# An S5 state-space layer beside a SwiGLU feed-forward layer: the last chunk's state output by seven block products, and the program's end in another order

## The chip, the core and the metric

The kernel runs on one core of a Trainium2 chip. The metric is device time in microseconds (us), lower is better. The engines are TensorE (PE in the profile, its weight loads PEld), VectorE (DVE), ScalarE (ACT), GpSimd (POOL) and SyncE (SP, which here only starts DMAs). Each engine runs its own instructions in order; what it needs from another engine it waits for.

## The reference

For 2048 rows `x` of 512 values, in bfloat16:

```python
xn = layernorm(x)
Lam_bar = exp(dt * Lam)                                  # Lam, B, C are complex, 512 states
h[t] = Lam_bar * h[t-1] + B_bar @ xn[t]                  # a recurrence over the 2048 rows
state = 2 * real(h @ C.T) + xn * Dskip
ffn = (silu(xn @ w_gate) * (xn @ w_up)) @ w_down         # 1376 features
out = x + state + ffn
```

## The kernel before

**Chunks and tiles.** The rows are worked in four chunks of 512 (`c` = 0 to 3), each of four tiles of 128 rows (`n` = 0 to 15). For a chunk the kernel projects to the states (`bproj_tile`), turns by the phase so that the recurrence becomes real (`rotation`, `rotation_dma`), scans along the rows on DVE (line 473, `g`), turns back into `wt` (real and imaginary part as two planes), and multiplies `wt` by `CF`, which holds the output matrix. `rotation_dma` does a part of the turning by DMAs that add into SBUF (line 438: `u<-pm`, `wt<-pm`). Beside this run the gate and up projections (line 508) into `gu_tiles[c]`, called `guT` in the profile, and their product on DVE (line 523).

**The output of a tile** is collected in one bank of PSUM, of which there are eight (`bank()`, tile name `ps`): ten matmuls of the feed-forward layer over 1280 features (`wd_sb`), three more over 32 rows of the array for the last 96 features (`out_rows`, with `gu_rows`), and the state output. `o_tiles[n]` is the list of the banks of tile `n`; `out_blocks` cuts one tile into column blocks of 256, 128 and 128, so that its stores can start one after the other.

**Seven products.** The state output of a chunk is a product of a 512 by 1024 matrix (`wt`, blocks `a11` to `a22`: time halves by planes) with a 1024 by 512 matrix (blocks `b11` to `b22`). For chunks 0, 1 and 2 `out_ssm_seven` makes it from seven block products instead of eight, with sums of blocks beforehand (`s1` to `s4` of `wt`, `t1` to `t4` of `CF`) and sums of products behind:

| name in the text | product | goes to |
|---|---|---|
| one | a11 b11 | own bank, copied to SBUF by ACT (line 731) |
| six | s2 t2 | own bank; six + one = u2 |
| five (`x`) | s1 t1 | own bank, copied to SBUF by ACT (line 734); five + u2 = low half, right |
| seven | s3 t3 | own bank; seven + u2 = high half, left; that + five = high half, right |
| low-left, high-left, low-right | a12 b21, a22 t4, s4 b22 | straight into the banks of the tiles |

Each product is eight matmuls 128x256. "Low" are a chunk's first two tiles, "high" the other two. The sums of products are DVE additions of 128x2x256 float32 (line 710). At the end DVE adds a tile's bank and the matching sum into `res`, which is stored. `skipped` adds `xn*Dskip + x`, kept in `xall`, to the sums of chunk 2 on POOL (line 717). Chunk 3 has no block sums: `out_ssm` multiplies the whole `wt` by `CF`, eight matmuls 128x512 a tile (line 815).

**The end of the program** is `out_pair(2)`, written out by hand: the feed-forward matmuls of all eight tiles of chunks 2 and 3 (line 779), their `out_rows`, the seven products of chunk 2, and then the plain state output of chunk 3, whose last tile (15) is cut in blocks. To free two banks before that, DVE first adds the banks of tiles 14 and 15 to `xn_end` and keeps them in `ends` (line 787). The block sums of chunk 2 (`state_sums(2)`: two copies on the ACT queue, four negations on ACT, four adding DMAs on the POOL queue) are started behind the first of the eight tiles.

**Order elsewhere.** Most of DVE's work for the recurrence waits in a list, `backlog`; `step()` issues its next item, `pump(us)` issues items as PE work of that length is recorded, `need(tag)` issues all up to a tag. `sums` is a second list, of which `spend(n)` issues up to cost `n` behind each gate and up tile.

Of the kernel before, what the change touches and what calls it, by code (L numbers as in the profile page):

```python
# [10 lines left out]
F32 = mybir.dt.float32  # L11
# [12 lines left out]
def kernel(  # L24
# [144 lines left out]
    part_end, jidx = ends[:, 0, :], ends[:, 1, :]  # L169
# [427 lines left out]

    def out_blocks(n):

        return ((0, D // 2), (D // 2, D - 128), (D - 128, D)) if n == NT - 1 else ((0, D),)  # L600

    def out_rows(c, step):

        for i in range(TPC):
            n, rows = c * TPC + i, slice(i * RT, (i + 1) * RT)
            nc.tensor.matmul(o_tiles[n][0][:], lhsT=gu_rows[c][rows, step, :], rhs=wd_rows[rows, step, :],  # L606
                             start=False, stop=(step == 2 and (c == 0 or n in parts)))
# [3 lines left out]
    parts = {NT - 1: part_end, NT - 2: jidx}  # L611
# [38 lines left out]
    def state_places(c):  # L650
        if c == 0:
            return halves(xnT, 0) + halves(xnT, 1)
        if c == 1:
            return [ssm.tile([128, NQ, HW], BF16, name="cm", bufs=3) for _ in range(2)] + halves(xnT, 2)
        return halves(wg_g[2], 0) + halves(wu_g[2], 0)

    def state_sums(c):

        (a11, a12), (a21, a22) = state_quarters(c)
        s1, s2, s3, s4 = s_tiles[c] = [t[:] for t in state_places(c)]  # L660
        q = nc.scalar if c == 2 else nc.sync
        if c == 0:
            yield from negated(s2, a22)
        yield from copied(s4, a12, q)
        yield from copied(s1, a21, q)
        yield from negated(s3, a21)
        yield from added(s3, a11)
        if c == 1:
            yield None
        if c:  # L670
            yield from negated(s2, a22)
        yield from added(s1, a22)
        if c == 0:
            yield None
        yield from added(s2, s3)
        yield from added(s4, s2)

    def out_ssm_seven(c, meanwhile=()):

        (a11, a12), (a21, a22) = state_quarters(c)  # L680
        (b11, b12), (b21, b22) = BQ
        (s1, s2, s3, s4), (t1, t2, t3, t4) = s_tiles[c], TQ
        first = c * TPC
        if c == 0:
            space = u_all[:].rearrange("p a b j -> p (a b j)").bitcast(F32).rearrange("p (s j) -> p s j", j=HD)
            spots = (0, 4)
            five = ssm.tile([128, D], F32, name="cm", bufs=3)[:].rearrange("p (i j) -> p i j", i=2)
        else:
            space = flat(gu_tiles[c][:]).bitcast(F32).rearrange("p (s j) -> p s j", j=HD)
            spots = (2, 6)  # L690
            five = space[:, 0:2]
        high, low = (space[:, a:a + 4].rearrange("p (i h) j -> p i h j", h=2) for a in spots)
        u2 = high[:, :, 1]

        def product(a, b, place, start, stop):
            for i in range(2):
                for q in range(NQ):
                    nc.tensor.matmul(place(i), lhsT=a[:, q, i * 128:(i + 1) * 128], rhs=b[:, q, :],  # L698
                                     start=(start and q == 0), stop=(stop and q == NQ - 1))

        def at(half, h):
            return lambda i: o_tiles[first + 2 * half + i][0][:, h * HD:(h + 1) * HD]

        def taken(a, b):
            x = bank((128, 2, HD))
            product(a, b, lambda i: x[:, i, :], True, True)
            return x

        def add(out, in0, in1):
            V.tensor_tensor(out=out, in0=in0, in1=in1, op=ALU.add)  # L710
            owed[0] -= 0.69

        def skipped(half, extra):
            if c == NCH - 2:
                lo = first + 2 * half
                sums = extra.rearrange("p i h j -> p i (h j)")
                nc.gpsimd.tensor_tensor(out=sums, in0=sums, in1=xall[:, lo:lo + 2, :], op=ALU.add)

        def finish(half, extra):
            for i in range(2):  # L720
                n = first + 2 * half + i
                res = opool.tile([128, D], BF16, name="res")
                add(res[:], o_tiles[n][0][:], extra[:, i].rearrange("p h j -> p (h j)"))
                if c == NCH - 2:
                    nc.sync.dma_start(out=out_v[:, n, :], in_=res[:])
                else:
                    nc.gpsimd.dma_start(out=out_v[:, n, :], in_=res[:], accum_op=ALU.add)  # L727

        product(a12, b21, at(0, 0), False, False)
        one = taken(a11, b11)  # L730
        nc.scalar.copy(out=low[:, :, 0], in_=one[:])  # L731
        six = taken(s2, t2)
        x = taken(s1, t1)
        nc.scalar.copy(out=five, in_=x[:])
        for _, op in meanwhile:
            op()

        def between():
            if c < NCH - 2:
                step()  # L740

        between()
        add(u2, six[:], low[:, :, 0])
        seven = taken(s3, t3)
        add(low[:, :, 1], u2, five)
        skipped(0, low)
        product(a22, t4, at(1, 0), False, c > 0)
        between()
        add(high[:, :, 0], seven[:], u2)
        add(high[:, :, 1], high[:, :, 0], five)  # L750
        skipped(1, high)
        product(s4, b22, at(0, 1), False, c > 0)
        if c == 0:
            for k in range(3):
                out_rows(c, k)
        between()
        if c == NCH - 2:
            finish(0, low)
            return lambda: finish(1, high)
        finish(1, high)  # L760
        finish(0, low)
        pump(4 * 2 * NQ * 0.2163)

    def out_pair(c):

        multiply(0)
        for n in [*parts, *range(c * TPC, NT - len(parts))]:
            o_tiles[n] = [bank()]
        for n in range(c * TPC, (c + 2) * TPC):
            if n == c * TPC + 1:  # L770
                need("skip")
                for _, op in filter(None, state_sums(c)):
                    op()
                skip_store(0)
                skip_store(1)
            o = o_tiles[n][0]
            k, i = divmod(n, TPC)
            for fi in range(FT - 1):
                nc.tensor.matmul(o[:], lhsT=gu_tiles[k][:, fi, i * 128:(i + 1) * 128], rhs=wd_sb[:, fi, :],  # L779
                                 start=(fi == 0), stop=False)  # L780
            pump(FT * 0.2163)
        for step in range(3):
            for k in (c, c + 1):
                out_rows(k, step)
        need(f"ssm{c + 1}")
        for n, part in parts.items():
            V.tensor_tensor(out=part, in0=o_tiles[n][0][:], in1=xn_end[:, n - NT + TPC, :], op=ALU.add)
        rest = out_ssm_seven(c)
        for n in range((c + 1) * TPC, (c + 2) * TPC):
            if n in parts:  # L790
                o_tiles[n] = [bank((128, hi - lo)) for lo, hi in out_blocks(n)]
            out_ssm(n)
            if n == NT - TPC:
                rest()

    def out_ffn(n):
        c, i = divmod(n, TPC)
        o_tiles[n] = []
        for lo, hi in out_blocks(n):
            o = bank((128, hi - lo))  # L800
            o_tiles[n].append(o)
            for fi in range(FT - 1):
                nc.tensor.matmul(o[:], lhsT=gu_tiles[c][:, fi, i * 128:(i + 1) * 128], rhs=wd_sb[:, fi, lo:hi],  # L803
                                 start=(fi == 0), stop=False)

    def out_ssm(n):
        c, i = divmod(n, TPC)
        if c > 0:
            res = opool.tile([128, D], BF16, name="res")
        for o, (lo, hi) in zip(o_tiles[n], out_blocks(n)):  # L810
            fresh = n in parts
            o = o[:, 0:hi - lo]
            for part in range(2):
                for q in range(NQ):
                    nc.tensor.matmul(o, lhsT=w_tiles[c][:, part, q, i * 128:(i + 1) * 128],  # L815
                                     rhs=CF[:, part, q, lo:hi], start=(fresh and part == 0 and q == 0),
                                     stop=(c > 0 and part == 1 and q == NQ - 1))
            if c == NCH - 1:
                rest = parts[n][:, lo:hi] if fresh else xn_end[:, i, lo:hi]
                V.tensor_tensor(out=res[:, lo:hi], in0=o, in1=rest, op=ALU.add)  # L820
# [367 lines left out]
```

## Time and profile before

| | |
|---|---|
| median of three runs | 176.35 us (176.21 to 176.76) |
| the profiled execution's own time | 176.91 us, of which the profile's span is 175.1 us |
| PE busy | 171.7 us, 98% of the span, granted clock 1.00 |
| DVE busy | 154.9 us, 88% |
| ACT busy | 100.3 us, 57% |
| POOL busy | 68.8 us, 39% |
| start of the feed-forward output matmuls of chunk 2 (line 779) | 140.44 us |
| last matmul's part of the chain ends | 172.44 us |

The profile is of one execution; it took 1.81 us more than its span, and lies 0.56 us above the median of the three runs. A row of the timeline gives the start, the length, the engine, the line and the operation with its tiles and shapes; in brackets stands how long the engine had been idle and what ended that. Matmuls overlap in the profile: one of 128x512 is shown with 379 ns, though the next starts 216 ns later. So a start is the better measure on PE, and a short wait doesn't show as idle time.

### The profile page before, as it was taken

To read this page: it belongs to the slowest core of one execution; us is meant where nothing else is said; L and a number is where in the kernel's file an instruction comes from. 1 tells how busy PE (TensorE), PEld (TensorE's weight loads), DVE (VectorE), ACT (ScalarE), POOL (GpSimd) and SP (SyncE) were. 2 spreads that over 40 slices of the span, in tenths; PEclk is the share of its full clock that TensorE was granted. 3 is DMA by queue.
4 is the path that set the end of the run, shared out by engine and by line. 5 is a ranking of instruction groups with operands and counts; after the bars stand their busy time and mean duration, and the time that the engine had idled before them with its cause. 6 is when DMAs were issued, how large, how long until landed. Compare 5 with 4: busy or idle time off the path is not lost.

```text
span 175.1 us, 2875 instructions
## 1 busy us (share of the span) xinstructions
PE 171.7 (98%) x1026; PEld 90.6 (52%) x1026; DVE 154.9 (88%) x223; ACT 100.3 (57%) x190; POOL 68.8 (39%) x87
## 2 busy tenths in 40 slices
PE   8999999999999999999999999999999999999993
PEld 3977644444444444444444584468444444447743
DVE  3778999999999998999999959997999999943884
ACT  5487899869997899199767760002297614001100
POOL 7050499312043314344520052595475003544440
DMA  5998498997574999999990669596999995949934
GB/s 170 300 164 210 95 260 118 340 198 150 106 212 144 172 168 247 190 140 124 115 117 7 181 88 105 64 140 112 170 135 197 159 146 132 105 53 131 173 99 140
DMA packets 45758, 26.61 MB, mean 152 GB/s; under 512 B 22272, under 2 KB 44544, under 8 KB 45728
## 3 DMA queue, kind: packets, MB, share of 16 engines
q0 software_dynamic: 12624, 11.67, 48.7%
q1 hardware_dynamic: 30672, 13.61, 34.6%
q10 hardware_dynamic: 2448, 1.15, 2.8%
q8 instruction: 8, 0.13, 0.3%
q14 instruction: 6, 0.05, 0.1%
HBM read 8.33 MB, written 4.19 MB: 71 GB/s over the span
## 4 chain that ended last, share of the span: by engine, by line
PE 98%; DVE 0%; issue 0%
PE ps L508 36%; PE ps L393 16%; PE ps L698 11%; PE ps L803 10%; PE ps L779 10%; PE ps L815 4%; PE ps L909 3%; PE ps L886 2%; PE ps L561 2%; PE ps L990 2%; PE ps L606 2%; PE ps L553 1%; PE ps L245 1%; DVE res L820 0%; PE ps L275 0%
## 5 line engine op out<-in xcount | busy, mean ns | idle before, releaser
L508 PE MATMUL ps<-xnT,wg 128*128 128x512 bf16 (+1 forms) x148 | 36.6, 373 | 0.0
L508 PE MATMUL ps<-xnT,wu 128*128 128x512 bf16 (+1 forms) x148 | 36.6, 373 | 0.0
L473 DVE TENSOR_TENSOR_SCAN g<-r_t,car,u 128x512 bf16<-128x512 f32 x24 | 29.1, 1266 | 0.0
L393 PE MATMUL ps<-xnT,BT 128*128 128x512 bf16 x128 | 28.3, 379 | 0.0
L527 ACT ACTIVATE guT<-ps 128x512 bf16<-128x512 f32 (+1 forms) x40 | 24.0, 601 | 6.4 <-PE ps L508 3.2
L528 ACT CAST u_all<-ps 128x512 bf16<-128x512 f32 (+1 forms) x40 | 23.3, 584 | 5.1 <-PE ps L508 4.8
L508 PEld LDWEIGHTS <-wu 128*128 128x128 bf16 x148 | 14.5, 98 | 16.6
L508 PEld LDWEIGHTS <-wg 128*128 128x128 bf16 x148 | 14.5, 98 | 16.5
L395 ACT CAST u<-ps 128x512 bf16<-128x512 f32 x32 | 18.3, 587 | 3.9 <-PE ps L393 3.7
L393 PEld LDWEIGHTS <-BT 128*128 128x128 bf16 x128 | 12.3, 98 | 15.2 <-issue 0.8
L803 PE MATMUL ps<-wd_sb,guT 128*128 128x512 bf16 x80 | 17.6, 379 | 0.0
L779 PE MATMUL ps<-wd_sb,guT 128*128 128x512 bf16 x80 | 17.4, 379 | 0.0
L731 ACT COPY guT<-ps 128x512 f32<-128x512 f32 x2 | 1.2, 585 | 27.0 <-PE ps L698 27.0
L523 DVE TENSOR_TENSOR guT<-guT,u_all 128x1024 bf16<-128x1024 bf16 x20 | 13.3, 677 | 0.0
L803 PEld LDWEIGHTS <-guT 128*128 128x128 bf16 x80 | 7.8, 98 | 9.6 <-issue 0.4
L779 PEld LDWEIGHTS <-guT 128*128 128x128 bf16 x80 | 7.8, 98 | 9.5
L205 DVE BATCH_NORM_STATS2 stats<-xall 128x6 f32<-128x512 bf16 x14 | 9.4, 674 | 2.7 <-DMA xall<-in_A_x_dram 2.7
L214 POOL TENSOR_TENSOR rstd<-ve,neg_half 128x2 f32<-128x2 f32 (+1 forms) x4 | 5.1, 1287 | 15.5 <-DVE ve L213 15.5
L625 POOL DMA_DIRECT2D xnT<-wt x3 | 3.9, 1287 | 15.2 <-DMA cm<-wt 12.0
L473 DVE TENSOR_TENSOR_SCAN g<-r_t,u 128x512 bf16<-128x512 f32 x8 | 9.3, 1204 | 0.0
L727 POOL DMA_DIRECT2D out_dram<-res x8 | 7.7, 1590 | 2.2 <-DVE res L710 2.2
L698 PEld LDWEIGHTS <-wt 128*128 128x128 bf16 x72 | 6.9, 98 | 1.8 <-issue 0.8
(180 smaller groups left out, 291.0 us busy)
## 6 DMA issues: line engine op xcount, KB each, us to landing
wt<-pm POOLq DMA_DIRECT2D x4, 512.0 KB, 5.7
u<-pm POOLq DMA_DIRECT2D x4, 512.0 KB, 6.3
wd_sb<-in_B_w_down_dram SPq DMA_DIRECT2D x2, 640.0 KB, 9.9
xall<-in_A_x_dram SPq DMA_DIRECT2D x1, 1024.0 KB, 6.7
out_dram<-res POOLq DMA_DIRECT2D x8, 128.0 KB, 4.9
out_dram<-xall POOLq DMA_DIRECT2D x2, 512.0 KB, 8.4
xnT<-wt SPq DMA_DIRECT2D x3, 256.0 KB, 3.7
xnT<-wt POOLq DMA_DIRECT2D x3, 256.0 KB, 7.0
```

What stands on the lines that cost most here:

```text
L205: nc.vector.bn_stats(out=stats[:, n, :], in_=xall[:, n, :])
L393: nc.tensor.matmul(ps[:], lhsT=BT[:, part, k, q * 128:(q + 1) * 128], rhs=xnT[:, k, c * CW:(c + 1) * CW], start=(k == 0), stop=(k == KD - 1))
L395: nc.scalar.copy(out=u_tiles[c][:, part, q, :], in_=ps[:])
L473: V.tensor_tensor_scan(out=g()[:, part, q, :], data0=r_t[:, q:q + 1].to_broadcast([128, CW]), data1=u_tiles[c][:, part, q, :], initial=ini ...
L508: nc.tensor.matmul(ps[:fs, lo:hi], lhsT=wslice(groups, fi, k), rhs=xnT[:, k, c * CW + lo:c * CW + hi], start=(k == 0), stop=(k == KD - 1))
L523: products.append(lambda: V.tensor_tensor(out=g, in0=g, in1=u, op=ALU.mult))
L527: nc.scalar.activation(out=gu_tile(c)[:, fi, 0:hi], in_=psg[:, 0:hi], func=ACT.Silu)
L528: nc.scalar.copy(out=u_tile(c, fi)[:, fi % 2, 0:hi], in_=psu[:, 0:hi])
L698: nc.tensor.matmul(place(i), lhsT=a[:, q, i * 128:(i + 1) * 128], rhs=b[:, q, :], start=(start and q == 0), stop=(stop and q == NQ - 1))
L727: nc.gpsimd.dma_start(out=out_v[:, n, :], in_=res[:], accum_op=ALU.add)
L779: nc.tensor.matmul(o[:], lhsT=gu_tiles[k][:, fi, i * 128:(i + 1) * 128], rhs=wd_sb[:, fi, :], start=(fi == 0), stop=False)
L803: nc.tensor.matmul(o[:], lhsT=gu_tiles[c][:, fi, i * 128:(i + 1) * 128], rhs=wd_sb[:, fi, lo:hi], start=(fi == 0), stop=False)
```

## The change

The state output of chunk 3 is made by seven block products like the other three chunks, and `out_pair` is replaced by `out_last`. In the new order PE does the feed-forward output of six tiles (the four of chunk 2, then 14 and 15 of chunk 3), then the products of chunk 2 and of chunk 3, the `out_rows` of both chunks, and last the feed-forward output of tiles 12 and 13. The tile cut in blocks is 13 (`LAST`) instead of 15.

The block sums of chunk 3 are four DVE additions (`state_sums_dve`), placed between DVE's sums of products. Those of chunk 2 are started earlier, during the gate and up projections of chunk 3: their two copies go to SP's queue, ahead of the twelve small DMAs that bring `gu_rows` of chunk 3, and their negations go between ACT's work for the gate and up tiles; they lie in `xnT` instead of `wg`/`wu`. `skip_add` and `skip_store` go behind some of them on POOL's queue. In all four chunks five stays in its bank and DVE reads it from there; ACT's copy of it is gone. In `out_ssm_seven(0)` one more `step()` is issued ahead of the first sum. The keeping of tiles 14 and 15 in `ends` is gone; tiles 14 and 15 keep their banks, and `skipped` is done for chunk 3 too.

```diff
     def state_sums(c):
...
+        if c == 2:
+            yield 1, lambda: None
+            yield from negated(s2, a22)
...
+    def state_sums_dve(c):
+        (a11, a12), (a21, a22) = state_quarters(c)
+        s1, s2, s3, s4 = s_tiles[c] = state_places(c)
+        for out, in0, in1, op in ((s3, a11, a21, ALU.subtract), (s1, a21, a22, ALU.add), (s2, s3, a22, ALU.subtract),
+                                  (s4, a12, s2, ALU.add)):
+            yield lambda out=out, in0=in0, in1=in1, op=op: V.tensor_tensor(out=out, in0=in0, in1=in1, op=op)
...
-        nc.scalar.copy(out=five, in_=x[:])
...
+        def add_low(self):
+            self.add(self.low[:, :, 1], self.p5[:], self.u2)
...
     def out_ssm_seven(c, meanwhile=()):
...
+        for _ in range(2 - c):
+            step()
+        p.add_six()
...
-    def out_pair(c):
+    def out_last(c):
         multiply(0)
+        need("skip")
+        late = [op for op in leftover if op]
+        for _, op in late[:1]:
+            op()
+        skip_store(2)
+        for _, op in late[1:]:
+            op()
+        skip_add()
+        skip_store(0)
+        skip_store(1)
+        lo, hi = c * TPC, (c + 1) * TPC
+        for n in (*range(lo, hi), hi + 2, hi + 3):
+            out_ffn(n)
             pump(FT * 0.2163)
+        need(f"ssm{c + 1}")
+        sums = state_sums_dve(c + 1)
+        p = Seven(c)
+        p.one()
+        p.six()
+        p.x()
+        next(sums)()
+        next(sums)()
+        p.add_six()
+        next(sums)()
+        p.seven()
+        p.add_seven()
+        p.add_low()
+        p.skipped(0)
+        p.add_high()
+        p.skipped(1)
+        p.low_left()
+        r = Seven(c + 1)
+        r.one()
+        r.six()
+        r.x()
+        next(sums)()
+        r.add_six()
+        r.seven()
+        r.add_seven()
+        r.add_low()
+        r.add_high()
+        r.skipped(1)
+        r.skipped(0)
+        p.high_left()
+        p.low_right()
         for step in range(3):
+            out_rows(c, step, closes=range(lo, hi))
+        for i in range(TPC):
+            p.finish(i)
+        open_tile(hi)
+        open_tile(LAST)
+        for step in range(3):
+            out_rows(c + 1, step, opens=(hi, LAST))
+        r.high_left(closes=True)
+        r.finish(2, (nc.scalar,), 2)
+        r.finish(3)
+        for i in range(2):
+            r.low_left(only=(i,))
+            r.low_right(only=(i,))
+        out_ffn(hi)
+        r.finish(0, (nc.scalar,))
+        out_ffn(LAST)
+        r.finish(1, (nc.scalar, nc.scalar, nc.sync))
...
     out_chunk(1)
+    need("ssm2")
+    third = state_sums(2)
+    sums += iter(lambda: next(third), None)
+    leftover[:] = third
     gateup_chunk(3)
-    out_pair(2)
+    spend(99)
+    out_last(2)
```

`p` is the product object of chunk 2 and `r` that of chunk 3; `finish(i)` is the last addition of the chunk's tile `i` and its store.

**DVE, its end, before.** From the last scans of chunk 3 (`g`) over the turning back into `wt` to the sums of products of chunk 2 (`guT`) and the last additions:

```order
L413 TENSOR_TENSOR wt<-pm 128x2048
L403 TENSOR_TENSOR pm<-g,c_91 128x2048
L417 TENSOR_TENSOR wt<-pm 128x2048
L787 TENSOR_TENSOR ends<-ps,xn_end 128x512 x2
L710 TENSOR_TENSOR guT<-ps,guT 128x2x256
L710 TENSOR_TENSOR guT<-guT 128x2x256
L710 TENSOR_TENSOR guT<-ps,guT 128x2x256
L710 TENSOR_TENSOR guT<-guT 128x2x256
L710 TENSOR_TENSOR res<-ps,guT 128x512 x2
```

**DVE, its end, now.** `wu` and `wg` are the block sums of chunk 3 in the order s3, s1, s2, s4; `guT` are sums of products of chunk 2 and `u` those of chunk 3:

```order
L417 TENSOR_TENSOR wt<-pm 128x2048
L699 TENSOR_TENSOR wu_82<-wt 128x4x256
L699 TENSOR_TENSOR wg_81<-wt 128x4x256
L743 TENSOR_TENSOR guT<-ps,guT 128x2x256
L699 TENSOR_TENSOR wg_81<-wu_82,wt 128x4x256
L743 TENSOR_TENSOR guT<-ps,guT 128x2x256 x3
L699 TENSOR_TENSOR wu_82<-wt,wg_81 128x4x256
L743 TENSOR_TENSOR u_1874<-ps,u_1874 128x2x256 x4
L743 TENSOR_TENSOR res<-ps,guT 128x512 x4
L743 TENSOR_TENSOR res<-ps,u_1874 128x512 x3
```

Two block sums now stand directly behind the last write of `wt` and ahead of the first sum of products, and a fourth stands ahead of chunk 3's first sum of products. The additions that emptied two banks into `ends` are gone.

**PE, the `out_rows` of chunk 3, now.** 1740 to 1780 are the banks of tiles 8 to 11, 1959 that of tile 12, 1960 to 1962 those of tile 13's blocks, 1795 and 1809 those of tiles 14 and 15; in brackets what the instruction waits for:

```order
L618 MATMUL ps_1780<-BT_88,gu_rows2_128 128x512
L618 LDWEIGHTS gu_rows3_129 [waits DMAHW1_49]
L618 MATMUL ps_1959<-BT_88,gu_rows3_129 128x512 [waits DVE_49]
L618 LDWEIGHTS gu_rows3_129 [waits DMAHW4_49]
L618 MATMUL ps_1960<-BT_88,gu_rows3_129 128x256 [waits DVE_49]
L618 LDWEIGHTS gu_rows3_129
L618 MATMUL ps_1961<-BT_88,gu_rows3_129 128x128 [waits DVE_49]
L618 LDWEIGHTS gu_rows3_129
L618 MATMUL ps_1962<-BT_88,gu_rows3_129 128x128 [waits DVE_49]
L618 LDWEIGHTS gu_rows3_129 [waits DMAHW7_49]
L618 MATMUL ps_1795<-BT_88,gu_rows3_129 128x512
```

**PE, the same place before.** 1736 is the bank of a tile of chunk 2, 1737, 1738, 1732 and 1731 those of tiles 12 to 15, all opened long before:

```order
L606 MATMUL ps_1736<-BT_88,gu_rows2_128 128x512
L606 LDWEIGHTS gu_rows3_129
L606 MATMUL ps_1737<-BT_88,gu_rows3_129 128x512
L606 LDWEIGHTS gu_rows3_129 [waits DMAHW4_49]
L606 MATMUL ps_1738<-BT_88,gu_rows3_129 128x512
```

The `out_rows` of tiles 12 and 13 now open four fresh banks in the middle of the end, and each of the four waits for DVE to empty it.

**POOL, its end, now.** The four `xnT` rows are the adding DMAs of chunk 2's block sums:

```order
L438 DMA u_1219<-pm 128x2048 x2
L636 DMA xnT<-wt 128x4x256 x2
L636 DMA xnT<-xnT 128x4x256
L592 DMA xall<-in_A_x_dram 128x4x512
L636 DMA xnT<-xnT 128x4x256
L587 DMA xn_end<-xall 128x2048
L594 DMA out_dram<-xall 128x4x512 x2
L775 TENSOR_TENSOR guT<-guT,xall 128x1024 x2
L775 TENSOR_TENSOR u_1874<-u_1874,xn_end 128x1024 x2
```

Before, the two DMAs of `xn_end` and `xall` stood ahead of the four adding DMAs, and there were two additions at the end instead of four.

More of the change, by code (lines that the diff above doesn't have):

```diff
@@ L730, in out_ssm_seven, with one, six, x @@
[L730 to L734, printed above, removed]
+        def one(self):
+            one = self.own(self.a11, self.b11)
+            nc.scalar.copy(out=self.low[:, :, 0], in_=one[:])
+        def six(self):
+            self.p6 = self.own(self.s[1], self.t[1])
+        def x(self):
+            self.p5 = self.own(self.s[0], self.t[0])
+        def seven(self):
+            self.p7 = self.own(self.s[2], self.t[2])
@@ L735, in out_ssm_seven @@
+    def out_ssm_seven(c, meanwhile=()):
+        p = Seven(c)
[3 more added lines that the diff above has]
+        p.x()
         for _, op in meanwhile:
             op()
[L738 to L749, printed above, removed]
@@ L750, in out_ssm_seven @@
-        add(high[:, :, 1], high[:, :, 0], five)
-        skipped(1, high)
-        product(s4, b22, at(0, 1), False, c > 0)
+        for _ in range(2 - c):
[3 more added lines that the diff above has]
+        p.add_low()
+        p.high_left(closes=c > 0)
+        step()
+        p.add_seven()
+        p.add_high()
+        p.low_right(closes=c > 0)
         if c == 0:
             for k in range(3):
[L755 to L759, printed above, removed]
@@ L760, in out_ssm_seven @@
-        finish(1, high)
-        finish(0, low)
+                out_rows(c, k, closes=range(TPC))
+        step()
+        for i in (2, 3, 0, 1):
+            p.finish(i)
         pump(4 * 2 * NQ * 0.2163)
-    def out_pair(c):
+    def out_last(c):
         multiply(0)
[L767 to L780, printed above, removed]
-            pump(FT * 0.2163)
-        for step in range(3):
[L783 to L794, printed above, removed]
@@ L806, in out_ssm @@
[L806 to L820, printed above, removed]
-                for a, b in ((0, D // 2), (D // 2, D)) if i == 0 else ((lo, hi),):
-                    late = b == D and n in (NT - TPC, NT - 1)
-                    (nc.sync if late else nc.scalar).dma_start(out=out_v[:, n, a:b], in_=res[:, a:b])
-            elif c > 0:
-                out_leave(n, o, res)
```

158 lines of the change are left out of this document (94 added, 64 removed).

## The prediction

> **What bounds the kernel now.** I read the page first, then the chain of waits for the last 35 us, then the timeline of the engines there. The page's first part:
>
> ```profile
> PE 171.7 (98%) x1026; PEld 90.6 (52%) x1026; DVE 154.9 (88%) x223; ACT 100.3 (57%) x190; POOL 68.8 (39%) x87
> ```
>
> The chain of waits from 140 us on (start, length, engine, tile and line):
>
> ```profile
> 140.44 17.27 PE ps L779 x80
> 157.71 1.41 PE ps L606 x24
> 159.12 6.36 PE ps L698 x56
> 165.47 6.96 PE ps L815 x48
> 172.44 0.02 issue
> 172.46 0.29 DVE res L820
> ```
>
> PE sets the end: 32.00 us from 140.44 to 172.44 without a stop that the chain shows, then one short addition and a store. So the change is worth what it does to PE's instructions, plus every wait that it puts into PE's row. Such a wait is there already, too short for the chain. The timeline around the products of chunk 2:
>
> ```profile
> 159.05 1.92 PE L698 MATMUL ps<-CF,wt 128*128 128x256 bf16 x16
> 160.81 1.91 PE L698 MATMUL ps<-CT,wg 128*128 128x256 bf16 x16
> 161.00 0.58 ACT L731 COPY guT<-ps 128x512 f32<-128x512 f32 x1 [13.93 <-PE ps L698]
> 161.95 0.69 DVE L710 TENSOR_TENSOR guT<-ps,guT 128x512 f32<-128x512 f32 x1 [1.49 <-PE ps L698]
> 162.69 1.03 PE L698 MATMUL ps<-CT,wu 128*128 128x256 bf16 x8
> ```
>
> Sixteen matmuls from 159.05 to 160.81 are 0.110 us each, 0.88 a product. Six and five start at 160.81, so six is through at 161.69, and seven could start at 162.57. It starts at 162.69, 0.05 after DVE's sum of six ends (162.64): six banks hold tiles, two are left for the products, and seven takes the bank that six leaves. A sum starts 0.26 after its product's last matmul. From these two steps follow all waits below.
>
> **PE's own work.** Prices: 17.27/80 = 0.216 a matmul of the feed-forward output; 1.41/24 = 0.059 of the `out_rows`; line 815's 48 are 24 of 512 columns (5.18), 8 of 256 (0.88), and so 16 of 128 in 0.90, 0.056 each. After: 70 of 512 columns 15.11; tile 13 in blocks, 10 x 0.110 + 20 x 0.056 = 2.22; the products 108 x 0.110 + 8 x 0.056 = 12.33; `out_rows` of chunk 2 0.71, and of chunk 3 eighteen, because tile 13 needs three where others need one: between 0.71 (beside the others) and 1.06 (one by one), taken 0.9. Sum 31.27 against 32.00: **-0.73** (-0.92 to -0.57). That is all that the saved product brings; the order costs more.
>
> **The waits that the new order makes.** Chunk 2's products start two tiles and all `out_rows` earlier: one begins at 140.44 + 60 x 0.216 = 153.39, seven could begin three products later, at 156.03. What DVE does till then:
>
> ```profile
> 133.08 0.68 DVE L523 TENSOR_TENSOR guT<-guT,u_all 128x1024 bf16<-128x1024 bf16 x1
> 133.68 2.35 DVE L584 TENSOR_TENSOR xall<-xall,dsk_bc 128x2048 bf16<-128x2048 bf16 x2
> ...
> 153.81 1.22 DVE L417 TENSOR_TENSOR wt<-pm 128x2048 bf16<-128x2048 bf16 x1
> 159.17 1.29 DVE L787 TENSOR_TENSOR ends<-ps,xn_end 128x512 f32<-128x512 f32 x2 [4.13 <-PE ps L606]
> ```
>
> Before, DVE had finished `wt` at 155.03 and then sat idle for 4.13 us; this slack is what the change spends. Now s3 and s1 stand there, each the size of line 523's product, 0.60 from start to start, so the sum of six runs from 156.23 to 156.92, and
> - **seven** starts at 156.97, a wait of 0.94. Everything else on PE is queued behind it. It ends at 157.85, low-left at 158.73.
> - **one of chunk 3** takes seven's bank, free when DVE has added seven: 157.85 + 0.26 + 0.69 + 0.05 = 158.85, a wait of 0.12. It ends at 159.73.
> - **six of chunk 3** takes five's bank, free after the two further sums, 0.61 apart: 160.08, a wait of 0.35. It ends at 160.96, five of chunk 3 at 161.84.
> - **seven of chunk 3** needs the bank that six leaves, and its sum stands behind s4 on DVE. Here a row of POOL decides:
>
> ```profile
> 163.98 0.68 DVE L710 TENSOR_TENSOR guT<-ps,guT 128x512 f32<-128x512 f32 x1
> 164.15 2.13 POOL L717 TENSOR_TENSOR guT<-guT,xall 128x1024 f32<-128x1024 f32 x1 [4.40 <-DVE guT L710]
> 164.70 2.13 DVE L710 TENSOR_TENSOR guT<-guT 128x512 f32<-128x512 f32 x1
> 166.75 1.28 DVE L710 TENSOR_TENSOR res<-ps,guT 128x512 bf16<-128x512 f32 x2
> 166.90 2.12 POOL L717 TENSOR_TENSOR guT<-guT,xall 128x1024 f32<-128x1024 f32 x1 [0.63 <-DVE guT L710]
> ```
>
> A DVE addition with both inputs in SBUF, started beside POOL's addition, took 2.13 instead of 0.69 us and ended 0.55 behind POOL's; those with one input in PSUM took 0.68 and 0.64. The sums now read PSUM and are safe, but s4 reads SBUF twice. POOL starts `skipped(0)` 0.09 behind the low sum (which ends at 159.42), at 159.51, and ends at 161.64; s4, ready at 159.95, ends at 162.19; the sum of six follows till 162.88, and seven starts at 162.93: a wait of 1.09. Were s4 not held, it would be 0.12. It ends at 163.81, high-left and low-right at 165.57, `out_rows` of chunk 2 at 166.28.
> - **`out_rows` of chunk 3** open four banks. Two are free; the third and fourth are those of tiles 8 and 9, which only now are complete. DVE's two `finish` additions take 0.61 + 0.69, so the fourth is free at 167.63, and all later matmuls stand behind it: about 1.2 of waiting, and no earlier DVE helps.
>
> Sum: 0.94 + 0.12 + 0.35 + 1.09 + 1.2 = 3.7, less 0.73: **+3.0 us**.
>
> The Trainium skill, page "SBUF — State Buffer", section "Who interferes with whom", says that a DVE instruction with two SBUF inputs and a GpSimd instruction that reads SBUF share one port pair, and that the second to issue is blocked until the first is done. By this rule s4 is held for one POOL addition, as in the row above (2.13 beside 2.13), and goes ahead of the second, which issues later; the sum stays +3.0.
>
> **When DVE has `wt`.** The first term hangs on 155.03. Two things move it:
>
> ```profile
> 102.45 0.69 DVE L710 TENSOR_TENSOR u_all<-ps,u_all 128x512 f32<-128x512 f32 x1 [1.19 <-PE ps L698]
> 103.87 0.69 DVE L710 TENSOR_TENSOR u_all<-u_all,cm 128x512 f32<-128x512 f32 x1 [0.73 <-ACT cm L734]
> 118.93 0.69 DVE L710 TENSOR_TENSOR guT<-ps,guT 128x512 f32<-128x512 f32 x1 [0.18 <-PE ps L698]
> 120.35 0.69 DVE L710 TENSOR_TENSOR guT<-guT 128x512 f32<-128x512 f32 x1 [0.73 <-ACT guT L734]
> ...
> 129.59 0.87 POOL L438 DMA_DIRECT2D u<-pm  x1 [0.51 <-DVE pm L432]
> 130.85 0.86 POOL L438 DMA_DIRECT2D u<-pm  x1 [0.39 <-DVE u L435]
> 135.96 1.27 DVE L473 TENSOR_TENSOR_SCAN g<-r_t,car,u 128x512 bf16<-128x512 f32 x1
> ```
>
> The extra scan fills the 1.19 and the waits of 0.73 for ACT's copy go, but at 118.93 DVE waits for chunk 1's six all the same, so only the second 0.73 counts: five is through a product after six, its sum starts about 0.6 earlier. Against that, SP's two copies of 256 KB enter the DMA engines just ahead of the two `u<-pm`, whose data chunk 3's scans need:
>
> ```profile
> u<-pm POOLq DMA_DIRECT2D x2, 512.0 KB, 6.1
> wg<-wt ACTq DMA_DIRECT2D x1, 256.0 KB, 3.9
> ...
> 120.00:125.00 5.00, 5.00 (x36) 3.23 (x34) 4.62 (x6) 1.48 (x3) 1.51 (x2) 1.00 0.80 150
> 130.00:135.00 5.00, 5.00 (x25) 2.27 (x24) 5.00 (x7) 3.99 (x8) 3.49 (x4) 1.00 1.06 186
> ```
>
> 129.59 + 6.1 = 135.7 against the scan at 135.96: almost no slack, and the engines are full (share 1.06, 186 GB/s). At that rate 512 KB are 2.8 us. If all of it delays the scans, `wt` comes 2.8 - 0.6 = 2.2 later; if the copies fit into the free 0.20 of 120 to 125, it comes 0.6 earlier. The first copy can start when the first `wt<-pm` has landed, inside that stretch, and the second not: I take +0.2 (bounds -0.6 and +2.2). That makes **+3.2**.
>
> **Moves that I cost at nothing.** ACT's four negations (0.58 each) stand between gate and up tiles, where ACT does 1.2 us of work in 1.73 of PE; without that cover they would delay banks of the next tiles. The adding DMAs of chunk 2's sums start about 134 and take 4.2 each, two behind each other before six of chunk 2, which needs s2 at 154.3: some 10 us of margin, also with the 512 KB of `xall` between; else PE would wait at six. SP's twelve `gu_rows` DMAs stand behind the copies but are wanted at 166 only. The tail behind the last matmul stays: the last block again has 128 columns and goes by SP.
>
> **The rivals.** *s4 is not held* (POOL late, or the port free): +3.2 - 0.97 = +2.2, 178.6; for it only that no bfloat16 addition beside a long POOL one is in the trace. *s4 is held by both POOL additions*, since the second needs nothing more by then and may start at once: 2.2 more, +5.4, 181.7; the rule of the skill speaks against it. *PE's clock falls.* All stretches show a granted clock of 1.00, but the first matmuls of the program are slow:
>
> ```profile
> L886 PE MATMUL ps<-const-bfloat16-1.0 128*128 128x512 bf16 x8 | 3.6, 628 | 0.8 <-PEq L1172 0.8
> ```
>
> 628 ns where later ones of this size show 379. If several waits bring this pace back for another 3.6 us, about half of it is lost: +1.8 more, 181.3. The Trainium skill, page "TensorE: Matmul & The Clock Gate", section "A second HAM failure mode: psum-queue depth-cycling", tells of a kernel that lost its clock by cycling through banks. Waits of about 1 us each between 3 us of work make it unlikely here. *Faster:* DVE empties every bank before PE asks, and the saved product counts alone: -0.73, 175.6. It needs the five waits to come to less than 0.73; DVE would have to have `wt` 0.9 earlier, s4 free of POOL, and tiles 8 and 9 drained in half a microsecond, where two additions need 1.3. *The waits nearly cancel the gain*: 176.3; the last wait alone is larger.
>
> **How the numbers follow.** Forecast 62 in 100: 176.35 + 3.2 = **179.5** on the median (the profiled execution's 176.91 would become 180.1; its span 178.3). s4 free 13, held twice 12, clock 5, faster 5, cancelled 3. The forecast's own range is 178.7 (`wt` 0.6 early) to 181.5 (2.2 late); with s4 free, `wt` early and the work at its lower bound it goes down to 177.6, with s4 held twice up to 181.7. So the range is 177.6 to 181.7. About 0.3% or 0.53 us is what a measurement of this kernel can tell from no change: faster 0.05, same 0.03, slower 0.92.
>
> **What would show it.** In the profile after: PE's share falls and gaps stand in its row ahead of seven of chunk 2 (0.9), six (0.35) and seven (1.1) of chunk 3, and inside line 618 (1.2), put down to DVE at line 743 or to bank waits; one block sum at line 699 takes over 2 us beside POOL's line 775; the feed-forward output of chunk 2 still starts at 140.4. Wrong would be: matmuls from 140.4 on without gaps and 31.3 us long, or a start that has itself moved.

## The result, and the profile after

The changed kernel takes **179.38 us** (median of 6 runs, 178.77 to 179.60) against 176.35 us (176.21 to 176.89) beside it: 1.016 times the time of before, 95% interval 1.0139 to 1.0181, that is 3.0 us slower. In a later set of rounds on one chip (experiment 8) it took 178.81 against 176.45, ratio 1.014 (1.0122 to 1.0157). The profiled execution took 179.60 us with a span of 177.8.

The page of the changed kernel, its engines, and below them the granted clock of its core:

```profile
PE 171.4 (96%) x1064; PEld 92.8 (52%) x1064; DVE 158.5 (89%) x229; ACT 98.7 (56%) x188; POOL 74.5 (42%) x89
...
core 0: 177.8 us, clock 1.000
```

PE's share falls from 98 to 96% while the page counts 38 more matmuls, and the granted clock is 1.000: PE does not run slower, it stands still. Where, the timeline of PE shows (start, busy time, line, operation, count; in brackets the idle time ahead and what ended it):

```profile
140.40 13.11 PE L891 MATMUL ps<-wd_sb,guT 128*128 128x512 bf16 x60
153.35 1.04 PE L722 MATMUL ps<-CF,wt 128*128 128x256 bf16 x8
154.22 1.91 PE L722 MATMUL ps<-CT,xnT 128*128 128x256 bf16 x16
156.39 1.03 PE L722 MATMUL ps<-CT,xnT 128*128 128x256 bf16 x8 [0.26 <-DVE guT L743]
157.26 1.04 PE L730 MATMUL ps<-CF,wt 128*128 128x256 bf16 x8
158.21 1.03 PE L722 MATMUL ps<-CF,wt 128*128 128x256 bf16 x8
159.53 1.91 PE L722 MATMUL ps<-CT,wg 128*128 128x256 bf16 x16 [0.29 <-DVE guT L743]
162.22 1.03 PE L722 MATMUL ps<-CT,wu 128*128 128x256 bf16 x8 [0.78 <-DVE u L743]
...
164.93 1.03 PE L618 MATMUL ps<-BT,gu_rows 32*128 32x512 bf16 x14
166.60 0.21 PE L618 MATMUL ps<-BT,gu_rows 32*128 32x128 bf16 x1 [0.64 <-DVE res L743]
167.19 0.83 PE L618 MATMUL ps<-BT,gu_rows 32*128 32x128 bf16 x15 [0.39 <-DVE res L743]
...
170.59 4.53 PE L891 MATMUL ps<-wd_sb,guT 128*128 128x512 bf16 x40
```

The rows are, from 153.35 on: one; six and five; seven; low-left of chunk 2; then one; six and five; seven of chunk 3; then the row matmuls. Each bracket stands where the prediction put a wait, and each names DVE's line 743, the sums that empty the banks. The brackets are short because a matmul's modelled end reaches into the idle time. They are measured from start to start instead, less what the matmuls take without a wait (0.875 us for eight, 1.75 for sixteen). So the waits are 0.42 (154.22 + 1.75 = 155.97, against 156.39), 0.07, 0.46 and 0.94, and inside the row matmuls, whose own step is 0.05, 0.95 and 0.55. Together 3.4 us.

DVE and POOL in the same stretch, in the timelines of the two:

```profile
153.31 1.22 DVE L417 TENSOR_TENSOR wt<-pm 128x2048 bf16<-128x2048 bf16 x1
154.45 0.68 DVE L699 TENSOR_TENSOR wu<-wt 128x1024 bf16<-128x1024 bf16 x1
155.05 0.68 DVE L699 TENSOR_TENSOR wg<-wt 128x1024 bf16<-128x1024 bf16 x1
155.66 0.68 DVE L743 TENSOR_TENSOR guT<-ps,guT 128x512 f32<-128x512 f32 x1
...
157.47 2.02 DVE L743 TENSOR_TENSOR guT<-ps,guT 128x512 f32<-128x512 f32 x3 [0.53 <-PE ps L722]
159.40 2.17 DVE L699 TENSOR_TENSOR wu<-wt,wg 128x1024 bf16<-128x1024 bf16 x1
161.48 0.68 DVE L743 TENSOR_TENSOR u<-ps,u 128x512 f32<-128x512 f32 x1
...
158.89 4.65 POOL L775 TENSOR_TENSOR guT<-guT,xall 128x1024 f32<-128x1024 f32 x2 [9.06 <-DVE guT L743]
```

`wt` ends at 154.53, then s3, s1 and the sum of six (till 156.34, seven starts at 156.39). The row of 2.17 us is s4 beside POOL's first addition; s3, s1 and s2, which also have two inputs in SBUF, take 0.68. The sum of six of chunk 3 stands behind it, and seven of chunk 3 behind that sum (162.16, start 162.22).

In the profile before, the last feed-forward output starts here:

```profile
140.28 17.43 PE L779 MATMUL ps<-wd_sb,guT 128*128 128x512 bf16 x80
```

From that first matmul to the end of the last one the profile before shows 32.16 us (140.28 to 172.44) and this one 34.72 (140.40 to 175.12): +2.6.

### The profile page after: what moved, and what is told of

Its sections match the earlier page's. It is cut to its first block, busy times and chain, and to the rows that moved or that the text cites. A ratio compares the mean times of both kernels' runs of the same rounds, so it can differ in the third digit from the quotient of the medians.

```text
span 177.8 us, 2957 instructions
## 1 busy us (share of the span) xinstructions
PE 171.4 (96%) x1064; PEld 92.8 (52%) x1064; DVE 158.5 (89%) x229; ACT 98.7 (56%) x188; POOL 74.5 (42%) x89
## 5 line engine op out<-in xcount | busy, mean ns | idle before, releaser
L891 PE MATMUL ps<-wd_sb,guT 128*128 128x512 bf16 (+2 forms) x180 | 35.2, 355 | 0.0
L891 PEld LDWEIGHTS <-guT 128*128 128x128 bf16 x180 | 16.8, 98 | 18.0 <-issue 0.4
L636 POOL DMA_DIRECT2D xnT<-wt x5 | 6.5, 1401 | 16.9 <-DMA cm<-wt 11.9
L636 POOL DMA_DIRECT2D xnT<-xnT x4 | 5.1, 1280 | 12.5 <-DMA xnT<-wt 8.4
L775 POOL TENSOR_TENSOR guT<-guT,xall 128x1024 f32<-128x1024 f32 x2 | 4.7, 2342 | 9.1 <-DVE guT L743 9.1
L743 DVE TENSOR_TENSOR guT<-ps,guT 128x512 f32<-128x512 f32 x8 | 5.4, 688 | 2.7 <-PE ps L722 2.5
```

The costliest lines, as they stand in the source:

```text
L636: yield 0, lambda: nc.gpsimd.dma_start(out=out, in_=in_, accum_op=ALU.add)
L891: nc.tensor.matmul(o, lhsT=gu_tiles[c][:, fi, i * 128:(i + 1) * 128], rhs=wd_sb[:, fi, lo:hi], start=(fresh and fi == 0), stop=(not fresh ...
```

## The experiments

All are edits of the changed kernel's `out_last` unless said otherwise. The profiles' starts of product one lie anywhere from 152.5 to 153.4 us, also for the same kernel: in the changed kernel's first profile PE waits for a weight DMA and starts line 508 at 10.60 us, in experiment 8 at 9.78, and all that follows is as much later. So beside the medians stands what no start disturbs, the time from the first matmul of product one to the end of the last matmul, **the end part**: 21.77 us in the changed kernel (153.35 to 175.12) and again in experiment 8 (152.52 to 174.29).

| run | median us | ratio to before (95%) | end part us |
|---|---|---|---|
| changed kernel | 179.38 | 1.016 (1.0139 to 1.0181) | 21.77 |
| 1 s4 early | 178.51 | 1.0095 (1.0072 to 1.0117) | 21.07 |
| 2 rows apart | 178.37 | 1.0096 (1.0077 to 1.0115) | 20.92 |
| 3 front filled | 177.36 | 1.0047 (1.0030 to 1.0064) | 20.33 |
| 4 filled | 175.85 | 0.9956 (0.9939 to 0.9972) | 18.50 |
| 5 no POOL additions | 178.35 | 1.0117 (1.0100 to 1.0135) | 20.89 |
| 6 five copied | 179.52 | 1.0176 (1.0162 to 1.0191) | 22.39 |
| 7 filled, chunk 3 plain | 176.56 | 1.0006 (0.9993 to 1.0019) | 19.33 |
| 8 changed again | 178.81 | 1.0140 (1.0122 to 1.0157) | 21.77 |
| 9 five copied again | 179.58 | 1.0195 (1.0174 to 1.0216) | 22.39 |
| 10 filled, POOL sooner | 176.20 | 0.9993 (0.9979 to 1.0006) | 19.08 |

Runs 1 to 4, 5 to 7 and 8 to 10 shared a chip and the runs of before. The same kernel has 179.38 in one set and 178.81 in another, so differences of half a microsecond between medians of different sets prove little; the end part carries the argument.

**1. s4 ahead of POOL's additions.**

```diff
         p.add_six()
         next(sums)()
+        next(sums)()
         p.seven()
...
         r.x()
-        next(sums)()
         r.add_six()
```

> s4 of chunk 3 is formed on DVE directly behind s2, at about 156.9 us, ahead of POOL's two additions, and no longer behind them. Theory (POOL's addition holds a bf16 addition of two SBUF operands on DVE, and with it the sum of six of chunk 3 and the bank of product seven): s4 takes 0.6 to 0.7 us, against 2.17, the sum of six of chunk 3 starts about 0.3 us behind its product, product seven of chunk 3 waits at most 0.15 us against 0.94, and the time falls by 0.8 from 179.4 to 178.6. Rival (the 2.17 us belong to s4's own operands): s4 takes 2.17 us in its new place too, product seven of chunk 2 and the sums behind it come 1.5 us later, and the time rises to 180 to 181. Rival (the wait that goes comes back at the rows of chunk 3, since these wait for POOL's additions): 179.4.

Timelines of DVE, POOL and PE:

```profile
156.59 0.69 DVE L699 TENSOR_TENSOR wu<-wt,wg 128x1024 bf16<-128x1024 bf16 x1
...
158.62 4.21 POOL L775 TENSOR_TENSOR guT<-guT,xall 128x1024 f32<-128x1024 f32 x2 [9.69 <-DVE guT L743]
...
161.14 1.03 PE L722 MATMUL ps<-CT,wu 128*128 128x256 bf16 x8
```

s4 takes 0.69 us, seven of chunk 3 follows five with a wait of 0.14, and POOL's pair takes 4.21 instead of 4.65. The end part is 0.70 shorter, not 0.80: one of chunk 3 now waits 0.18 (0.07 before), since s4 delays the sum with seven. The wait does not come back at the rows (0.64 and 0.39 in the brackets, as in the changed kernel). Both rivals fall.

**5. POOL's two additions to chunk 2 left out,** s4 in its late place. The rows of chunk 2 then lack `xn*Dskip + x`.

```diff
-        p.skipped(0)
         p.add_high()
-        p.skipped(1)
```

> POOL's two additions of xn*Dskip + x to the sums of chunk 2 are left out (that part is missing in the rows of chunk 2); everything else is the changed kernel, s4 in its late place too. Theory (s4 waits for POOL's first addition to end and then takes its own 0.6 us): s4 takes 0.6 to 0.7 us at about 159.4, product seven of chunk 3 waits at most 0.2 us against 0.94, and the time falls by 0.8 from 179.4 to 178.6. Rival (s4's late place behind three other sums is what costs, whatever POOL does): 179.4.

```profile
158.61 0.68 DVE L699 TENSOR_TENSOR wu<-wt,wg 128x1024 bf16<-128x1024 bf16 x1
...
160.64 1.03 PE L722 MATMUL ps<-CT,wu 128*128 128x256 bf16 x8
```

In the same place behind the same sums, s4 takes 0.68 us once POOL is idle, and the end part loses 0.88. With 1 this shows POOL's addition, not s4's place or operands, as what held it.

**2. The upper left product of chunk 3 between the two sets of row matmuls.**

```diff
         for i in range(TPC):
             p.finish(i)
+        r.high_left()
         open_tile(hi)
         open_tile(LAST)
         for step in range(3):
-            out_rows(c + 1, step, opens=(hi, LAST))
-        r.high_left(closes=True)
+            out_rows(c + 1, step, opens=(hi, LAST), closes=(hi + 2, hi + 3))
```

> The upper left product of chunk 3 (8 matmuls, 0.87 us) stands between the row matmuls of chunk 2 and those of chunk 3. Theory (the last two blocks of tile 13 wait for DVE to finish tiles 8 and 9): PE works 0.87 us while DVE finishes them, of the 1.5 us that the row matmuls wait about 0.6 remain, and the time falls by 0.85 from 179.4 to 178.5. Rival (the row matmuls wait for something that starts only with them): their wait stays at 1.5 us and the time at 179.4.

PE's timeline:

```profile
164.53 0.83 PE L618 MATMUL ps<-BT,gu_rows 32*128 32x512 bf16 x12
165.29 1.05 PE L730 MATMUL ps<-CT,wt 128*128 128x256 bf16 x8
166.27 1.35 PE L618 MATMUL ps<-BT,gu_rows 32*128 32x512 bf16 x18
```

One block of 0.87 us of other work takes 0.85 us off the end part; the 18 row matmuls still take 1.35 against 0.83 in experiment 4, so part of the wait is left, as expected.

**3. Chunk 2's direct products as fillers in front.** A product that adds into its tile's own bank needs no free bank.

```diff
         next(sums)()
+        p.low_left()
+        p.add_low()
+        p.skipped(0)
         p.seven()
         p.add_seven()
-        p.add_low()
-        p.skipped(0)
         p.add_high()
         p.skipped(1)
-        p.low_left()
+        p.high_left()
...
-        p.high_left()
         p.low_right()
```

> Chunk 2's lower left product stands ahead of product seven and its upper left one behind it, and the sum with product five stands on DVE ahead of that with seven. s4 and the rows are as in the changed kernel. Theory (each wait is one bank that DVE frees too late, and 0.87 us of other work covers it): product seven waits 0 against 0.42 us, product one of chunk 3 about 0.1, products six and five of chunk 3 at most 0.1 against 0.46, product seven of chunk 3 still 0.8 to 1.0 (s4 held by POOL), the row matmuls still 1.5, and the time falls by 0.75 from 179.4 to 178.6. Rival (PE's waits are interchangeable: what is taken off in front comes back at product seven, since POOL's additions end when they did): 179.2 to 179.4.

PE, DVE and POOL:

```profile
158.73 1.91 PE L722 MATMUL ps<-CT,wg 128*128 128x256 bf16 x16
160.62 1.03 PE L722 MATMUL ps<-CT,wu 128*128 128x256 bf16 x8
...
163.76 0.26 PE L618 MATMUL ps<-BT,gu_rows 32*128 32x256 bf16 x1 [0.27 <-DVE u L743]
164.36 0.21 PE L618 MATMUL ps<-BT,gu_rows 32*128 32x128 bf16 x1 [0.33 <-DVE res L743]
...
158.45 1.09 DVE L699 TENSOR_TENSOR wu<-wt,wg 128x1024 bf16<-128x1024 bf16 x1
...
156.87 4.66 POOL L775 TENSOR_TENSOR guT<-guT,xall 128x1024 f32<-128x1024 f32 x2 [8.51 <-DVE guT L743]
```

The waits at seven of chunk 2 and six of chunk 3 are gone, as expected. The end part fell by 1.44, twice what was expected, because I had left s4's hold unchanged: with the low sum earlier, POOL started 4.32 us behind product one's first matmul (156.87 - 152.55) instead of 5.54 (158.89 - 153.35), 1.2 sooner, and s4 met only the last half microsecond of its first addition. It took 1.09 us, and seven of chunk 3 waits 0.14. In return the rows now wait three times (the third has 0.39 in its bracket).

**4. All three, and chunk 2 finished ahead of chunk 3.**

```diff
+        p.high_left()
+        p.low_right()
+        for step in range(3):
+            out_rows(c, step, closes=range(lo, hi))
         r = Seven(c + 1)
         r.one()
         r.six()
         r.x()
+        for i in range(3):
+            p.finish(i)
         r.add_six()
+        p.finish(3)
         r.seven()
-        r.add_seven()
         r.add_low()
+        r.skipped(0)
+        r.add_seven()
         r.add_high()
         r.skipped(1)
-        r.skipped(0)
-        p.high_left()
-        p.low_right()
-        for step in range(3):
-            out_rows(c, step, closes=range(lo, hi))
-        for i in range(TPC):
-            p.finish(i)
```

Ahead of this stand the edits of 1 and 3 (with them `high_left` had already moved), behind it that of 2.

> All three together, and chunk 2's remaining products and row matmuls ahead of chunk 3's first product, so that DVE and POOL have four groups of PE work in which to free banks. Theory (all that the changed kernel lost are waits for banks, 0.42 + 0.07 + 0.46 + 0.94 + 0.1 + 1.5 + 0.2 = 3.7 us, and no work was added on PE): PE has no wait over 0.2 us behind 153.35 us, the time falls by 3.3 to 3.7 to 175.7 to 176.1, which is 0.2 to 0.6 below the kernel before. Rival (the waits move to POOL's four additions, 2.1 us each, behind which the four finished tiles of chunk 2 stand on DVE): PE waits 1 to 2 us at products five and seven of chunk 3 and the time is 177 to 178.

PE's timeline, the last feed-forward output and then chunk 2's row matmuls and what follows (one record of each feed-forward group is missing):

```profile
139.57 13.11 PE L892 MATMUL ps<-wd_sb,guT 128*128 128x512 bf16 x59
...
158.73 0.83 PE L618 MATMUL ps<-BT,gu_rows 32*128 32x512 bf16 x12
159.49 1.05 PE L722 MATMUL ps<-CF,wt 128*128 128x256 bf16 x8
160.38 1.91 PE L722 MATMUL ps<-CT,wg 128*128 128x256 bf16 x16
162.12 1.04 PE L722 MATMUL ps<-CT,wu 128*128 128x256 bf16 x8
163.00 1.04 PE L730 MATMUL ps<-CT,wt 128*128 128x256 bf16 x8
163.96 0.83 PE L618 MATMUL ps<-BT,gu_rows 32*128 32x512 bf16 x18
...
166.72 4.31 PE L892 MATMUL ps<-wd_sb,guT 128*128 128x512 bf16 x39
```

No row has a bracket, and the starts follow each other at the products' own lengths: the view shows no wait of PE. The same work that took 21.77 us takes 18.50, and the kernel beats the one before (0.9956, 0.9939 to 0.9972). So the waits for banks are what the changed kernel lost: 3.4 us by its profile, 3.3 by this run. From the first feed-forward matmul to the end of the last one it takes 31.46 us (139.57 to 171.03), 0.70 less than the kernel before. DVE does wait for POOL's additions there (0.97 and 0.81 us in its timeline), but no bank is missed meanwhile.

**7. The filled order with the eight plain products for chunk 3.** `eight(n)` is the inner loop of the old `out_ssm`; chunk 3's sums fall away, and `finish` adds `xn_end` instead.

```diff
-        r.one()
...
-        r.high_left()
+        eight(hi + 2)
+        eight(hi + 3)
...
-            r.low_left(only=(i,))
-            r.low_right(only=(i,))
+            eight(hi + i)
```

> The order of the filled kernel, but chunk 3's state output by the eight plain products again (32 matmuls of 512 columns' worth, 6.9 us, against 56 of 256 columns, 6.1 us), with xn*Dskip + x added when the tile is finished, and none of chunk 3's sums. Theory (the seven products save PE 0.73 to 0.83 us, and in the filled order nothing of it is given back): the time is 0.7 to 0.8 above the filled kernel's 175.85, that is 176.6 to 176.7, where the kernel before is. Rival (the gain of the filled kernel is its order alone, and the sums of the seven products cost as much as the product saves): 175.7 to 176.0.

PE and POOL:

```profile
158.74 0.83 PE L618 MATMUL ps<-BT,gu_rows 32*128 32x512 bf16 x12
159.72 3.40 PE L822 MATMUL ps<-CF,wt 128*128 128x512 bf16 x15 [0.16 <-issue]
163.06 0.83 PE L618 MATMUL ps<-BT,gu_rows 32*128 32x512 bf16 x18
...
156.18 2.12 POOL L775 TENSOR_TENSOR guT<-guT,xall 128x1024 f32<-128x1024 f32 x1 [7.39 <-DVE guT L743]
```

Here too nothing holds PE up (the 0.16 us stand where the record of one matmul of sixteen is missing), and the time is 176.56, 0.71 above the filled kernel, and 0.83 more in the end part. The interval of its ratio to the kernel before holds 1: the order alone gains nothing that these runs show. The saved product is what the filled kernel gains.

**6 and 9. ACT's copy of product five put back in chunks 0 and 1.**

```diff
         def x(self):
             self.p5 = self.own(self.s[0], self.t[0])
+            if self.c < NCH - 2:
+                nc.scalar.copy(out=self.five, in_=self.p5[:])
...
-            self.add(self.low[:, :, 1], self.p5[:], self.u2)
+            self.add(self.low[:, :, 1], self.five if self.c < NCH - 2 else self.p5[:], self.u2)
```

> For chunks 0 and 1 ACT copies product five out of PSUM again, and the two sums with it read the copy, as in the kernel before; the rest is the changed kernel. Theory (DVE reached the last state weights 0.5 us earlier than before, 154.53 against 155.03, because its sums no longer wait 0.73 us for that copy, and product seven of chunk 2 waits for what DVE does next): measured from the first matmul of product one, the state weights end 0.4 to 0.6 us later, product seven waits 0.8 to 1.0 us against 0.42, and the time rises by 0.5 to 179.9. Rival (DVE's lead has another source, such as additions moved to DMAs): product seven's wait and the time stay, 179.4.

> The changed kernel again, as the base of the two runs beside it. The state weights end 1.2 us behind the first matmul of product one, product seven waits 0.4 us, and the time is 179.2 to 179.5.

> The kernel with product five of chunks 0 and 1 copied, once more, with the changed kernel on the same chip in the same rounds, since its profile showed the state weights 1.8 us behind product one's first matmul and a wait of 1.04 us at product seven, but its time stood only 0.1 over that of the changed kernel in other rounds. Theory (DVE's 0.6 us are on the path): 0.5 to 0.6 us slower than the changed kernel beside it. Rival (PE starts its last feed-forward output 0.6 us earlier by something else that the copy changes, which takes the wait back): within 0.2 us of it.

DVE and PE in run 6:

```profile
119.87 0.69 DVE L748 TENSOR_TENSOR guT<-guT 128x512 f32<-128x512 f32 x1 [0.73 <-ACT guT L761]
...
153.33 1.22 DVE L417 TENSOR_TENSOR wt<-pm 128x2048 bf16<-128x2048 bf16 x1
...
152.75 1.04 PE L727 MATMUL ps<-CF,wt 128*128 128x256 bf16 x8
...
156.41 1.03 PE L727 MATMUL ps<-CT,xnT 128*128 128x256 bf16 x8 [0.88 <-DVE guT L748]
```

The wait of 0.73 us for the copy, some 35 us ahead of the end of `wt` (119.87 against 154.55), is back, and `wt` ends 1.80 us behind product one's start (153.33 + 1.22 - 152.75) instead of 1.18 (154.53 - 153.35). Seven waits 1.04 instead of 0.42, and the end part is 0.62 longer in both runs. In run 6 the median showed only 0.14 of it, against rounds of another set; side by side, 9 is 0.77 above 8 (179.58 and 178.81). DVE's queue is that tight: from 119.87 to the end of `wt` its timeline marks no idle time, so the 0.62 us that it lost there arrive whole. Run 8 came in 0.4 below its own expected range in time, with the same end part and the same waits as the first profile; in its profile product one starts 0.83 earlier (152.52 against 153.35).

**10. The filled kernel with POOL's last additions sooner.**

```diff
         r.add_six()
+        r.add_low()
+        r.skipped(0)
         p.finish(3)
         r.seven()
-        r.add_low()
-        r.skipped(0)
```

> The filled kernel with DVE's sum of chunk 3's five ahead of the fourth finished tile of chunk 2, so that POOL's two additions to chunk 3 start 0.6 us sooner (163.8 for 164.4). Theory (in the filled kernel the last four finished tiles stand behind POOL, 168.68, and its four stores bunch at the end, with 2.6 us between DVE's last addition and the end of the span against 2.35 in the changed kernel): DVE finishes tile 14 at 168.1 and the time falls by 0.1 to 0.3, to 175.6 to 175.75. Rival (the end is PE's last matmul and the last store's own time): 175.85, no change.

```profile
162.38 1.48 DVE L743 TENSOR_TENSOR u<-ps,u 128x512 f32<-128x512 f32 x2
163.77 0.68 DVE L743 TENSOR_TENSOR res<-ps,guT 128x512 bf16<-128x512 f32 x1
...
164.50 0.82 PE L618 MATMUL ps<-BT,gu_rows 32*128 32x128 bf16 x15 [0.20 <-DVE res L743]
```

A miss: 176.20 for 175.85. POOL's additions did start sooner (163.99 for 164.43), but the sum with five now stood ahead of the fourth finished tile, behind the sum of six whose result it reads, and the finished tile started at 163.77 instead of 163.02. Five itself held nothing up: PE was through with it at 162.24. The last block of tile 13 takes that tile's bank, so the rows waited, and the end part grew by 0.58.

## Why the prediction was right, and where its sizes were off

The forecast was 179.5 and the time 179.38; that the two agree to 0.1 us is luck, as the sizes below show. The mechanism, PE waiting for banks that DVE frees, stands shown: experiment 4 takes the waits away and the time with them. The steps one by one:

- **PE's work, -0.73.** Experiment 4, in which PE waits for nothing, takes 31.46 us against 32.16 before: -0.70. Right. Experiment 7 against 4 prices the products of chunk 3 alone: 0.83 in the end part, 0.71 by the medians.
- **Start of the last feed-forward output.** 140.40 against 140.28. As forecast, but it lies at 139.57 in experiment 8 with the same kernel, so the agreement to 0.1 is chance.
- **seven of chunk 2, 0.94 and 0.2 for a late `wt`.** Measured 0.42. This is the step that was mis-sized most. The prediction had the two forces on `wt` right, and both ends of the range, but set SP's two copies against the saved wait at +0.8. They cost nothing: the scan that waits for the `u<-pm` DMAs stands without a bracket right behind its neighbour:

```profile
133.18 2.35 DVE L584 TENSOR_TENSOR xall<-xall,dsk_bc 128x2048 bf16<-128x2048 bf16 x2
135.45 1.27 DVE L473 TENSOR_TENSOR_SCAN g<-r_t,car,u 128x512 bf16<-128x512 f32 x1
```

  That leaves the saved wait for five alone. `wt` ended 14.13 us behind the feed-forward start (154.53 - 140.40) against 14.75 before (155.03 - 140.28): 0.62 earlier, the lower bound; experiments 6 and 9 give the same 0.62.
- **one of chunk 3, 0.12; six, 0.35.** 0.07 and 0.46. Right in kind, 0.1 off.
- **seven of chunk 3, 1.09, of which 0.97 by POOL.** 0.94, with s4 at 2.17 us. Experiments 1 and 5 take 0.80 of it away with the hold (0.14 left). Right in kind, 0.15 too long. The rule that the prediction took from the Trainium skill, page "SBUF — State Buffer", section "Who interferes with whom", held: s4 was blocked until the POOL instruction that issued first was done. POOL's two additions to chunk 2, with the lengths in ns (smallest, median, largest):

```profile
L775 POOL TENSOR_TENSOR guT<-guT,xall x2: 2120/2342/2565, 158.9 to 161.0; 128x1024 f32<-128x1024 f32 x2
```

  The first took 2.12 us and ended at 158.89 + 2.12 = 161.01, and s4 0.56 later, at 161.57. The second, started at 161.0, took 2.57 instead of the 2.12 that it takes unheld (experiment 7), which fits the prediction's conclusion that s4 goes ahead of the second. In experiment 3 the same sum gives 156.87 + 2.12 = 158.99, and s4 ended at 159.54. The rivals "not held" and "held by both" fall.
- **the rows of chunk 3, 1.2.** 0.95 + 0.55 = 1.5: the fourth bank came free 0.3 later against the rows than I reckoned. The working starts DVE's two additions right at the end of chunk 2's rows (166.28) and leaves out the 0.26 us from a last matmul to its sum, which it counts for the products; the first of these additions started at 165.85, and the rows of chunk 2 ended, from start to start, at 165.59. Experiment 2 covers 0.85 of the wait.
- **The clock.** The granted clock is 1.000, and eight matmuls of a product still take 0.87 us from start to start between the waits. The waits of up to a microsecond cost no pace, so the failure that the prediction cited from the Trainium skill, page "TensorE: Matmul & The Clock Gate", section "A second HAM failure mode: psum-queue depth-cycling", is not what happened here.

With the measured sizes the prediction's sum is 3.4 - 0.73 = +2.7, and the two profiles differ by +2.6 from the feed-forward start on. The medians differ by 3.0 in one set of rounds and by 2.4 in the other. So the 179.5 was closer to the first median than its working deserved: the wait of seven of chunk 2 was 0.7 too long with its late `wt`, the rows 0.3 too short, and the 0.4 between the 2.6 of the profiles and the 3.0 of the first medians stays open; two profiles of the same kernel lie 0.8 apart before product one starts.

## What to carry to other kernels

Where products of one size pass through two accumulators, each wait is the time from a product's end to its freed bank less the work that stands between; order the products so that those that add into a bank already held stand between those that need a new one. Here that turned a loss of 2.6 us into a gain of 0.7. Before putting more on an engine with slack, follow its queue back as far as it runs without idling: here 0.62 us lost some 35 us ahead reached the end whole. An addition with two inputs in SBUF belongs ahead of a long GpSimd addition, not beside it (0.69 us against 2.17 here).

## What was not expected of the hardware

Two plain copies of 256 KB, moved into a stretch where the DMA engines' busy share was 0.80 to 1.06 before, delayed nothing that DVE waited for. And moving POOL's work 1.2 us earlier was worth as much to seven of chunk 3 as taking s4 out of its way (a wait of 0.14 in both): what counts is which part of POOL's instruction the other one meets (s4 took 1.09 us where it met the last half microsecond, 2.17 where it met the last 1.6, 0.69 alone).
